# Fourteen dummy matmuls instead of twelve ahead of the first x tile, in a TensorE-bound state-space and expert kernel

## The chip, the cores and the metric

The kernel runs on one core of one Trainium2 chip. The metric is the device time of one execution in microseconds (us). The kernel before took 247.78 us (median of three runs, 247.73 to 248.76).

## The reference, cut to what matters

```python
x = A_x                                              # 1 x 2048 x 1024
g = sigmoid((x * gate_w).sum(-1))
a = ssm(x)        # diagonal complex recurrence over 2048 steps:
                  #   Bu = x @ B_bar^T (real and imaginary plane), h_t = Lam_bar * h_{t-1} + Bu_t
                  #   y  = 2 Re(h @ C^T) + x * Dskip
b = experts(x)    # the 8 tokens with the largest x @ w_r go through a gated MLP; added back to x
return g * a + (1 - g) * b
```

The bulk of the work is two large matrix products: x with the two planes of B (tile `vps`, line 269), and the states with the two planes of C (tile `zps`, line 765). The inputs are bf16. x and B have to be transposed on the way in.

## The kernel before

The large loads of the start are issued from one queue, SyncE's, in this order; only the second plain x tile and the small vectors go through other queues. x is worked on in blocks of 512 rows. The first half of block 0 (two tiles of 128 rows) comes in plain and is transposed on TensorE; the rest of x, B and C are transposed by the DMA.

```python
for tl in range(BPC):                                   # L77: x tiles 0 and 1, plain
    (nc.scalar if tl else nc.sync).dma_start(x0r[:, tl, :], x2d[tl * P:(tl + 1) * P, :])
load_B(0, 0, 1)                                         # L80: real plane of B, row block 0
...
new_X(0)
load_xT(1)                                              # L92: second half of x block 0
load_B(1, 0, 1)                                         # L80: imaginary plane, row block 0
for c0, c1 in ((1, 2), (2, 3), (3, 4), (4, 6), (6, 8)): # the other row blocks, both planes
    for pl in range(2):
        load_B(pl, c0, c1)
```

While the x tiles are on their way, TensorE has nothing to do and multiplies zeros into a PSUM tile that nothing reads. That is the warm-up. It is meant to have TensorE's clock open early. I read the clock from the distance between the starts of two neighbouring 128x256 matmuls: 0.21 us for the dummies in the profile before (the clock is slow, or "cold") and 0.11 us from the first real matmuls on (it is "open").

```python
def warm(n):
    for _ in range(n):
        nc.tensor.matmul(wps[:], lhsT=wt0[:, 0:P], rhs=wt0[:], start=True, stop=True)   # L152, 128x256

warm(12)
for tl in range(BPC):
    ...
    for dc in range(KD):                                # L159: 16 transposes
        nc.tensor.transpose(xq[:, dc, :], x0r[:, tl, dc * P:(dc + 1) * P], ident[:])
    (nc.scalar.copy if tl == 0 else nc.vector.tensor_copy)(out=X[0][...], in_=xq[:])    # L160
warm(2)
... # the three small vectors, L164
warm(1)
s1u(0, 0, 0, 0, 1)    # 8 matmuls: real plane, first half of x
warm(2)
s1u(0, 0, 0, 1, 2)    # 8: real plane, second half of x
s1u(0, 0, 1, 0, 2)    # 8: imaginary plane, both halves
...                   # then two small transposes (vb_ps, L434), then row blocks 1 to 7
```

## Time and profile before

| | before |
|---|---|
| span of the profiled execution | 245.8 us |
| TensorE busy | 239.3 us (97%) |
| VectorE busy | 225.8 us (92%) |
| TensorE waits of more than 0.1 us, all | 1.1 (start), 0.3 (x tile), 0.2 (issue), 0.5 us (B's imaginary plane) |

The span is the time from the first to the last instruction; the device time is some 2 us longer. TensorE is the bound from about 11 us on, so what a change of the start is worth is read from the moment at which TensorE gets into its continuous stream. I use one marker for it: the start of the two small `vb_ps` transposes (L434). They stand in the program right after the first 24 real matmuls (16 of half width and 8 of full width). In the profile before they start at 11.06 us, which leaves 245.8 - 11.06 = 234.7 us for the rest.

### The profile page before, as it was taken

How to read it: one execution, taken by the hardware profiler on the slowest of the kernel's cores; microseconds unless marked ns; L12 is line 12 of the kernel's file. 1: busy time of each engine (PE TensorE's matmuls, PEld its weight loads, DVE VectorE, ACT ScalarE, POOL GpSimd, SP SyncE). 2: the span in 40 equal slices, each digit the busy share in tenths (PEclk: the TensorE clock that was granted, in tenths of full speed). 3: DMA queues.
4: the chain of work that ended last, by engine and by line, in shares of the span. 5: the costliest groups of instructions: out<-in, count | busy, mean ns of one | idle time of the engine just before them, and what ended most of it. 6: DMA issues, size and time to landing. Idle time of an engine off the chain costs nothing.

```text
span 245.8 us, 3504 instructions
## 1 busy us (share of the span) xinstructions
PE 239.3 (97%) x1355; PEld 112.8 (46%) x1379; DVE 225.8 (92%) x229; ACT 119.3 (49%) x205; POOL 26.9 (11%) x47
## 2 busy tenths in 40 slices
PE   7999999999999999999999999999999999999994
PEld 5544444444444444444444444444444444447453
DVE  0889999999999999999999999999999999999952
ACT  3599993233463472323355462235266445456421
POOL 4000000000000300720002030100100211110210
PEclk9999999999999999999999999999999999999999
DMA  8999999999750260577156999778699999942052
GB/s 192 204 156 226 238 237 255 202 241 296 241 169 0 105 153 0 97 160 225 77 192 219 343 264 325 217 239 299 191 347 327 389 293 300 147 65 37 2 132 85
DMA packets 65313, 48.48 MB, mean 197 GB/s; under 512 B 50560, under 2 KB 52224, under 8 KB 65296
## 3 DMA queue, kind: packets, MB, share of 16 engines
q1 hardware_dynamic: 59968, 37.20, 57.8%
q0 software_dynamic: 3264, 7.38, 13.8%
q10 hardware_dynamic: 2064, 3.68, 4.3%
q8 instruction: 11, 0.18, 0.3%
q14 instruction: 6, 0.05, 0.1%
HBM read 27.55 MB, written 8.40 MB: 146 GB/s over the span
## 4 chain that ended last, share of the span: by engine, by line
PE 94%; DMA 2%; SPq 2%; issue 1%; DVE 0%
PE vps L269 44%; PE zps L765 42%; PE zps L781 3%; PE pgu L657 3%; DMA BT<-in_A_B_im_dram 2%; PE y L669 1%; SPq L92 1%; PE zr L483 1%; SPq L80 1%; DVE ot L786 0%; SPq L77 0%; PE xselT_ps L570 0%; PE zs_ps L586 0%; PE zt L490 0%; PE vb_ps L434 0%
## 5 line engine op out<-in xcount | busy, mean ns | idle before, releaser
L269 PE MATMUL vps<-X,BT 128*128 128x512 bf16 (+1 forms) x508 | 111.2, 376 | 1.2 <-DMA BT<-in_A_B_im_dram 0.5
L765 PE MATMUL zps<-CT,H 128*128 128x512 bf16 x469 | 104.4, 379 | 0.6
L269 PEld LDWEIGHTS <-BT 128*128 128x128 bf16 x520 | 50.2, 98 | 60.3 <-issue 1.0
L765 PEld LDWEIGHTS <-H 128*128 128x128 bf16 x480 | 46.5, 98 | 56.6 <-issue 1.3
L306 DVE TENSOR_TENSOR_SCAN U<-d,U 128x2048 bf16<-128x2048 f32 (+2 forms) x22 | 62.0, 2860 | 1.0 <-DVE U L297 0.5
L276 ACT CAST V<-vps 128x512 bf16<-128x512 f32 x64 | 34.3, 588 | 57.7 <-PE vps L269 55.3
L770 ACT ACTIVATE ot<-zps,gcol 128x512 bf16<-128x512 f32 x30 | 20.6, 687 | 46.0 <-PE zps L765 44.8
L739 ACT CAST zps<-xd 128x512 f32<-128x512 bf16 (+1 forms) x29 | 16.6, 576 | 3.9 <-ACT xt L726 2.9
L296 DVE TENSOR_TENSOR V<-V,nTi 128x4096 bf16<-128x4096 bf16 (+2 forms) x11 | 16.7, 1516 | 0.5
L295 DVE TENSOR_TENSOR U<-V,T2tab 128x4096 bf16<-128x4096 bf16 (+2 forms) x11 | 16.6, 1509 | 0.5
L297 DVE TENSOR_TENSOR U<-U,V 128x4096 bf16<-128x4096 bf16 (+2 forms) x11 | 16.7, 1516 | 0.4
L791 POOL DMA_DIRECT2D out_dram<-ot x14 | 13.0, 928 | 30.6 <-ACT ot L770 28.6
L331 DVE TENSOR_TENSOR U<-U,S2tab 128x4096 bf16<-128x4096 bf16 x7 | 16.0, 2292 | 0.2
L333 DVE TENSOR_TENSOR H<-H,U 128x4096 bf16<-128x4096 bf16 x7 | 16.0, 2291 | 0.2
L726 ACT ACTIVATE xt<-xt,omgcol 128x1024 bf16<-128x1024 bf16 x14 | 16.0, 1144 | 0.0
L329 DVE TENSOR_TENSOR H<-U,Ctab 128x4096 bf16<-128x4096 bf16 x7 | 16.0, 2284 | 0.0
L703 POOL DMA_DIRECT2D xt<-in_A_x_dram x12 | 7.2, 596 | 80.6 <-ACT ot L770 22.2
L364 DVE TENSOR_TENSOR_SCAN U<-D,U 128x1024 bf16<-128x1024 f32 x4 | 8.9, 2279 | 0.1
L721 DVE TENSOR_TENSOR xd<-xt,Dbc 128x1024 bf16<-128x1024 bf16 x14 | 9.0, 684 | 0.0
L657 PE MATMUL pgu<-wgu,xsel 128*32 128x448 bf16 x128 | 7.2, 354 | 0.1
L781 PE MATMUL zps<-CT,H 128*128 128x256 bf16 (+1 forms) x47 | 7.1, 307 | 0.1
L716 POOL DMA_DIRECT2D out_dram<-xt x2 | 1.5, 755 | 49.6 <-ACT zps L739 49.6
(152 smaller groups left out, 128.6 us busy)
## 6 DMA issues: line engine op xcount, KB each, us to landing
wgu<-in_B_w_gate_dram SPq DMA_DIRECT2D x16, 448.0 KB, 3.7
wgu<-in_B_w_up_dram SPq DMA_DIRECT2D x16, 448.0 KB, 5.8
out_dram<-ot POOLq DMA_DIRECT2D x14, 256.0 KB, 5.6
wdb<-in_B_w_down_dram SPq DMA_DIRECT2D x7, 512.0 KB, 10.4
xt<-in_A_x_dram POOLq DMA_DIRECT2D x12, 256.0 KB, 4.4
out_dram<-xt ACTq DMA_DIRECT2D x12, 256.0 KB, 5.7
wd<-in_B_w_down_dram SPq DMA_DIRECT2D x5, 512.0 KB, 8.0
xt<-in_A_x_dram SPq DMA_DIRECT2D x4, 256.0 KB, 4.0
```

The costliest lines, as they stand in the source:

```text
L269: nc.tensor.matmul(o, lhsT=BT[pl][:, dc, ct * P:(ct + 1) * P], rhs=X[m][:, dc, k0 * LC:k1 * LC], start=(dc == 0), stop=(dc == KD - 1))
L276: nc.scalar.copy(out=V[k][:, :, ct, :], in_=vp[m, ct][:, :, kk, :])
L295: nc.vector.tensor_tensor(out=u, in0=v, in1=T2tab[:, :, c0:c1, :], op=ALU.mult)
L296: nc.vector.tensor_tensor(out=v, in0=v, in1=bc(nTi, c0, c1), op=ALU.mult)
L297: nc.vector.tensor_tensor(out=u, in0=u, in1=V[k][:, ::-1, c0:c1, :], op=ALU.add)
L306: nc.vector.tensor_tensor_scan(out=fl, data0=d0[:, c0:c1, :].rearrange("p c t -> p (c t)"), data1=fl, initial=0.0, op0=ALU.mult, op1=ALU.add)
L329: nc.vector.tensor_tensor(out=h, in0=g, in1=bc(Ctab, c0, c1), op=ALU.mult)
L331: nc.vector.tensor_tensor(out=g, in0=g, in1=S2tab[:, :, c0:c1, :], op=ALU.mult)
L333: nc.vector.tensor_tensor(out=h, in0=h, in1=G[k][:, ::-1, c0:c1, :], op=ALU.add)
L739: nc.scalar.copy(out=z[:], in_=xd[b][:, d_:d_ + w])
L765: nc.tensor.matmul(zps[:], lhsT=H[k][:, pl, ct, tl * P:(tl + 1) * P], rhs=CT[pl][:, ct, dsl], start=(fresh and ct == 0 and pl == 0), stop= ...
L770: nc.scalar.activation(out=ots[b][:, dsl], in_=zps[:], func=ACT.Copy, scale=gcol[:, b:b + 1])
```

## The change

The intent is to keep TensorE busy until the first x tile has landed, so that no hole is left between warm-up and transposes.

```diff
-    warm(12)
+    warm(14)
```

## The prediction

> **What bounds the kernel now.** I read the chain that ended last first, because it says which engine sets the end and when that engine last waited for something else. Its columns are start (us), length (us), and what.
>
> ```profile
> 0.74 0.40 SPq L77
> ...
> 1.21 1.31 SPq L80
> 2.52 0.05 issue
> 2.57 2.41 SPq L92
> 4.98 0.04 issue
> 5.02 4.16 DMA BT<-in_A_B_im_dram
> 9.18 0.27 issue
> 9.45 1.67 PE vps L269 x7
> ...
> 20.05 10.74 PE vps L269 x49
> ...
> 242.63 0.48 DVE ot L786
> ```
>
> From 9.45 us to about 242.6 us the chain is matmuls on TensorE and short instruction-issue gaps; nothing else stands in it until the last VectorE instruction. Ahead of 9.45 us there is no TensorE work in it at all: there the chain is the SyncE queue issuing loads one after another (x tile, first B transpose, x transpose) and then the landing of the imaginary plane of B, issued at 5.02 us and landed 4.16 us later, at 9.18 us. So the kernel is two pieces: a front of 9.45 us set by loads, and a TensorE-bound rest. Then the waits of TensorE over the whole span (line, what it waited for, us in total, times, longest):
>
> ```profile
> PE wps L152 <- DVE halfpi L132: 1.1, 1, 1.1
> PE vps L269 <- DMA BT<-in_A_B_im_dram: 0.5, 1, 0.5
> PE xq L159 <- DMA x0r<-in_A_x_dram: 0.3, 1, 0.3
> PE vps L269 <- issue: 0.2, 1, 0.2
> ```
>
> These four are all of them. The third is the hole that the change fills, 0.3 us until the x tile has landed. The second comes after it, in front of the real matmuls: TensorE stands still for 0.5 us until B's imaginary plane lands. [...] Last, the timeline of TensorE in the first 9.5 us (start, length, engine, line, operation, tiles, shape, count, idle before):
>
> ```profile
> 1.06 2.74 PE L152 MATMUL wps<-wt 128*128 128x256 bf16 x12 [1.06 <-DVE halfpi L132]
> 4.10 1.89 PE L159 MATMUL xq<-ident,x0r 128*128 128x128 bf16 x16 [0.30 <-DMA x0r<-in_A_x_dram]
> 6.52 0.29 PE L152 MATMUL wps<-wt 128*128 128x256 bf16 x1
> 6.87 1.03 PE L269 MATMUL vps<-X,BT 128*128 128x256 bf16 x8
> ...
> 9.45 0.38 PE L269 MATMUL vps<-X,BT 128*128 128x512 bf16 x1 [0.46 <-DMA BT<-in_A_B_im_dram]
> ```
>
> The first row is the warm-up, the second the 16 transposes of the x tile. They start when the tile lands, not when the warm-up ends. The last row shows the 0.46 us before the first matmul that needs B's imaginary plane.
>
> **What the Trainium skill says.** (1) "Perfetto Trace Analysis", section "Per-instruction lifecycle", for TensorE: the profiled end of a matmul is an estimate that includes the write to PSUM. So a dummy costs the distance to the next start, not its printed duration. The trace agrees: a dummy lasts 418 ns by its row (median of 17), but the first of the twelve starts at 1.06 us and the twelfth at 3.38 us, which is 2.32 / 11 = 0.211 us apart. (2) "TensorE: Matmul & The Clock Gate", Part 1: start-to-start is N / 1.2 GHz while the array is cold and N / 2.4 GHz + 2.5 ns once warm, so for N = 256 an estimate of 213 and 109 ns. The trace agrees on both: 211 ns in the warm-up, and (7.63 - 6.87) / 7 = 109 ns between the first and the eighth start of the first real group. The clock row of the page reads full speed in all forty slices; here I believe the start-to-start distances. (3) The same Part 1: the clock opens after a busy window of about 3.4 us, and the window runs free of the kernel's start. In this trace the dummy at 6.00 us still lasts 0.42 us and the one at 6.52 us lasts 0.29 us, the warm form, so the clock opened between them. (4) The same page, Part 4, says that transposes do not engage the fast clock in the way matmuls do. The transposes here run at (5.7 - 4.1) / 15 = 0.107 us, the cold rate, but the clock opened shortly after, so the trace does not decide it.
>
> **The change part by part.** It removes nothing. It adds two weight loads and two 128x256 matmuls on TensorE, right after the twelve. The comparison of the instruction orders of the two kernels shows no other change on any engine but renumbered tiles: same loads, same queue order, same positions of everything after. The dummies write a PSUM tile that nothing reads; the one instruction that waits for the last dummy of the kernel is a GpSimd memset at 8.18 us, which waits for a later dummy (7.74 us).
> Cost: two matmuls at the cold distance, 2 x 0.211 = 0.42 us of TensorE. Where they lie: the twelfth starts at 3.38 us, so the thirteenth starts at 3.59, the fourteenth at 3.80, and the array takes the next instruction at 4.01 us. The transposes start at 4.10 us because of the load. So 0.42 us of work goes into a hole that by starts is 4.10 - 3.59 = 0.51 us wide (the 0.30 us of the row is counted from the estimated end of the twelfth). About 0.09 us is left: the delay of the transposes is 0, or at most some 0.1 us if the x tile lands earlier than in this execution.
> Sum to the end of the span: 0 from the transposes, and if there is a delay of 0.1 us, it has to pass the wait of 0.46 us at 9.45 us, which nothing on TensorE sets. That leaves 0 for the matmul part of the path. The other way to the end is through the copies of the x tile and the small vectors to VectorE, which is busy 92% of the span. A shift of 0.1 us there would be felt only if TensorE waited for VectorE later, and it does not once in 233 us. So the expected change is 0.0 us.
>
> **The rivals.** (a) The warm-up outlasts the tile. If the load lands 0.2 us earlier in some executions, or if the loads of weights make each dummy dearer, the transposes start 0.1 to 0.3 us late. Against it: the 0.211 us is steady over twelve. Even then the 0.46 us covers it: change 0, at worst +0.1 us. (b) The clock opens earlier. With the hole filled, the 3.4 us window before the transposes holds more work, and in some phases of the window the clock would open at about 4.3 us instead of 7.7. Then 16 transposes take 16 x 0.056 = 0.9 us (the warm figure for N = 128 of Part 1) in place of 1.7, and X is there up to 0.8 us earlier. This is surely what the change is for. For it speaks that the clock is still slow until past 6 us here. Against it: the real matmuls that follow still meet the load that lands at 9.18 us, so TensorE just waits longer, 1.3 us in place of 0.5. Change 0. (c) The clock opens late, in the worst phase at about 1.06 + 2 x 3.4 = 7.9 us. From the timeline, the 16 real half-width matmuls before the wait need 16 x 0.109 = 1.7 us warm and 16 x 0.211 = 3.4 us cold. With the clock opening at 7.9 only the first group of 8, which starts at 6.87 us, would be partly cold: about 5 at 0.211, so some 0.5 us more, just what the wait of 0.46 us covers. If the clock stayed shut through 9.4 us, the front would be about 1.7 - 0.5 = 1.2 us longer, 249.0 us. That is a tail which both kernels have and which the change makes slightly rarer. One of the three runs of before, 248.76, is 1.0 us above the median; I can't tell from one trace if this is it. (d) The two added instructions move the places where TensorE stops for instruction issue, the 0.05 us pieces after every 49 matmuls. Their number does not change: within 0.05 us.
>
> **Range and chances.** All of (a), (b) and (d) end at 0 to 0.1 us; (c) is spread that before has as well. So the predicted time is that of before, 247.8 us. The range is the spread between runs and not the change: three runs of before lie from 247.73 to 248.76, and a median of a few runs in another session may move by some 0.2%. I take 247.3 to 248.5. Two per cent is 5 us, half of the whole front, and the change touches 0.4 us: faster 0.005, same 0.99, slower 0.005.
>
> **What would show it right or wrong.** Right: fourteen dummies from about 1.06 us to about 4.2 us by the rows, transposes starting within 0.1 us of 4.10, no wait for the x tile or one under 0.1 us, the first full-width matmul still at about 9.4 us right after B's imaginary plane lands, and the same 233 us from there to the end. Step (a) is wrong if the transposes start after 4.2 us with the tile long landed. Step (b) shows if the transposes are 0.056 us apart and the wait before 9.4 us has grown by as much. The prediction is wrong if the first full-width matmul moves with the transposes, or if TensorE has a wait for VectorE or ScalarE after 10 us that before had not, or if the load of B's imaginary plane lands at another time than 9.18 us by more than 0.3 us because of the change and not by chance.

## The result, and the profile after

| | before | after |
|---|---|---|
| median, six runs each in the same rounds | 247.55 us | 247.47 us |
| lowest to highest | 246.91 to 248.76 | 247.17 to 247.55 |
| span of the profiled execution | 245.8 us | 245.6 us |
| start of the vb transposes | 11.06 us | 10.76 us |
| rest of the span | 234.7 us | 234.8 us |

The ratio is 0.999 with a 95% interval of 0.9966 to 1.0014. A ratio is the mean time of one kernel's runs over that of the other's of the same rounds, so it is not quite the ratio of the medians in the table.

First TensorE's timeline of the changed kernel for the first 11 us (start, length, engine, line, operation, tiles, shape, count, idle before).

```profile
1.06 3.17 PE L152 MATMUL wps<-wt 128*128 128x256 bf16 x14 [1.06 <-DVE halfpi L132]
4.21 1.89 PE L159 MATMUL xq<-ident,x0r 128*128 128x128 bf16 x16
5.89 0.59 PE L152 MATMUL wps<-wt 128*128 128x256 bf16 x2
...
6.98 1.03 PE L269 MATMUL vps<-X,BT 128*128 128x256 bf16 x8
...
8.06 2.76 PE L269 MATMUL vps<-X,BT 128*128 128x256 bf16 x16
10.76 0.20 PE L434 MATMUL vb_ps<-ident,vrow 8*128 8x8 bf16 x2
```

The fourteen dummies are there and the hole is gone from the matmul rows. The transposes start 0.11 us later than before (4.21 against 4.10 us), and the first row of real matmuls too. But the last group before the vb transposes now runs through: the wait of 0.46 us for B's imaginary plane is gone.

Did the dummies push the transposes? The matmul row cannot tell, because it shows no idle time once the modelled ends overlap. The weight loads can. Here is their timeline in the same window, the kernel before first, then the changed one:

```profile
1.06 2.26 PEld L152 LDWEIGHTS <-wt 128*128 128x128 bf16 x12 [1.06 <-DVE halfpi L132]
4.10 0.98 PEld L159 LDWEIGHTS <-x0r 128*128 128x128 bf16 x10 [0.78 <-DMA x0r<-in_A_x_dram]
```

```profile
1.06 2.69 PEld L152 LDWEIGHTS <-wt 128*128 128x128 bf16 x14 [1.06 <-DVE halfpi L132]
4.21 0.88 PEld L159 LDWEIGHTS <-x0r 128*128 128x128 bf16 x9 [0.45 <-DMA x0r<-in_A_x_dram]
```

In both, the weight load of the first transpose waited for the x tile. The wait shrank from 0.78 to 0.45 us. In this execution the tile simply landed later, 3.4 us after its issue instead of 3.3. So the two dummies lay in the hole and pushed nothing. Nor is this one lucky execution: the fourteenth dummy leaves the array free at 3.81 + 0.21 = 4.02 us, and in all fourteen profiles the first x tile landed at 4.02 to 4.27 us.

Next the chain that ended last in the changed kernel (start, length, what):

```profile
1.06 3.17 PE wps L152 x14
4.23 1.88 PE xq L159 x16
...
6.14 0.69 DVE X L160
...
6.98 1.03 PE vps L269 x8
8.01 0.22 PE wps L152 x2
8.23 2.60 PE vps L269 x16
10.83 0.13 PE vb_ps L434 x2
10.96 48.53 PE vps L269 x224
```

The chain no longer leads through the queue of loads and B's imaginary plane. It leads through the x tile, the transposes, VectorE's copy of the tile and then matmuls. (That it begins with the dummies is an effect of the modelled ends; the weight loads above show the wait for the tile.) The plane of B was issued at 5.14 us and landed 3.4 us later, at about 8.6 us, which is before TensorE wanted it (its first matmul starts at 8.94 us). In the profile before it was 5.02 + 4.16 = 9.18 us. Is that the change, or chance? Nothing in the change touches this load, but that is an argument and not a measurement, so it was the first question for the experiments.

The last row also corrects a reading. There are 224 matmuls in 48.53 us, 0.2167 us each, and no "issue" pieces between them. The pieces of 0.05 us after every 49 matmuls in the profile before were records missing from that trace: (10.74 + 0.05) / 0.2167 = 49.8, so fifty matmuls were there. The header counts say the same: 1355 TensorE instructions before, 1381 after, for a change that adds two. A later look at the unchanged kernel has 1379, and none of these pieces.

### The profile page after: what moved, and what is told of

Same layout as the page of the kernel before. It is cut to its first block, busy times and chain, and to the rows that moved or that the text cites. A ratio compares the mean times of both kernels' runs of the same rounds, so it can differ in the third digit from the quotient of the medians.

```text
span 245.6 us, 3532 instructions
## 1 busy us (share of the span) xinstructions
PE 241.2 (98%) x1381; PEld 113.1 (46%) x1381; DVE 225.8 (92%) x229; ACT 119.1 (48%) x205; POOL 26.8 (11%) x47
## 4 chain that ended last, share of the span: by engine, by line
PE 98%; DVE 1%; issue 0%
PE vps L269 45%; PE zps L765 42%; PE zps L781 3%; PE pgu L657 3%; PE wps L152 1%; PE y L669 1%; PE xq L159 1%; PE zr L483 1%; DVE X L160 0%; DVE ot L786 0%; PE xselT_ps L570 0%; PE zs_ps L586 0%; PE zt L490 0%; DVE wt L129 0%; PE vb_ps L434 0%
```

## The experiments

Twelve kernels were run, timed in up to five rounds beside the kernel before on the same chip. Two theories stood at the start. Mine: the dummies lie in a hole, and what moves the front from execution to execution is the landing of loads and the moment at which the clock opens. The rival: the change itself moved something (the landing of B, or the clock) and is worth 0.1 to 0.3 us.

### 1. The kernel before against itself, and the changed kernel again

No edit in either.

> The kernel before, unchanged, timed against itself: the noise floor. Theory (the dummies fill a hole and the front is set by loads whose landing varies): ratio 1.000 within 0.002, and the profile lands B's imaginary plane somewhere between 8.4 and 9.3 us, with the start of the first full-width matmul either at about 8.9 us (landing before it is needed) or 0.27 us after the landing. Rival (the change itself moved that landing from 9.18 to 8.5 us): the landing is again at 9.1 to 9.2 us here.

> The changed kernel again. Theory: ratio 0.998 to 1.001; the transposes start with the landing of the x tile (4.1 to 4.2 us), the clock opens at about 6.3 us, the landing of B's imaginary plane anywhere from 8.4 to 9.3 us. Rival (the change is a real gain of 0.1 to 0.3 us by an earlier landing): ratio 0.9990 or less with the landing at 8.5 us again.

> One more look at the kernel before for where the clock opens and where the loads land. Theory (the time of opening is a matter of chance between 4.2 and 7 us): the transposes are either 0.107 or 0.056 us apart, and the span less the start of the vb transposes is 234.8 us within 0.1. Rival (twelve dummies always open it at the same time): as in the first look, 6.3 us.

Measured: the kernel before against itself gave 247.35 against 247.52 us, ratio 1.0003 (0.9965 to 1.0041). The changed kernel gave 247.58 us in the same rounds, ratio 0.9997 (0.9967 to 1.0027). So an interval of five rounds is about 0.7% wide here, and an effect of 0.1 us (0.04%) cannot be seen in times. It can be bounded in traces. TensorE's timeline of the first look at the unchanged kernel:

```profile
4.24 1.07 PE L159 MATMUL xq<-ident,x0r 128*128 128x128 bf16 x16 [0.44 <-DMA x0r<-in_A_x_dram]
...
6.18 1.03 PE L269 MATMUL vps<-X,BT 128*128 128x256 bf16 x8 [0.25 <-DVE vec L165]
7.05 0.38 PE L152 MATMUL wps<-wt 128*128 128x256 bf16 x2
7.38 1.03 PE L269 MATMUL vps<-X,BT 128*128 128x256 bf16 x8
8.94 1.67 PE L269 MATMUL vps<-X,BT 128*128 128x512 bf16 x7 [0.52 <-DMA BT<-in_A_B_im_dram]
10.54 0.20 PE L434 MATMUL vb_ps<-ident,vrow 8*128 8x8 bf16 x2
```

Here the sixteen transposes take 1.07 us instead of 1.89, so the clock was open at 4.24 us, with twelve dummies. B's imaginary plane landed at 8.67 us (issued at 5.22, 3.44 us to land). In the second look (state unknown, being a single run) the plane landed in time, at 8.65 us, and the transposes were slow again:

```profile
4.22 1.89 PE L159 MATMUL xq<-ident,x0r 128*128 128x128 bf16 x16 [0.42 <-DMA x0r<-in_A_x_dram]
...
8.08 2.76 PE L269 MATMUL vps<-X,BT 128*128 128x256 bf16 x16
10.77 0.20 PE L434 MATMUL vb_ps<-ident,vrow 8*128 8x8 bf16 x2
```

What follows: the early landing of B comes without the change, so the rival is refuted on that point. Of the thirteen profiles that load B's first row block in this order, with whatever number of dummies, eleven have the plane landed at 8.39 to 8.84 us. The late ones are the profile before (9.18) and that of joinB below (9.51), two of the seven with twelve dummies, too few to tie a late landing to the number of dummies. The moment at which the clock opens varies by some 2 us between executions of one and the same kernel (before 4.24 us in the first look; in the second, dummies at 5.90 and 6.12 us are still 0.21 us apart). And in the first look it is seen what an early clock is worth: the real matmuls start at 6.18 instead of 6.87 us, then TensorE waits for B all the same, 0.52 us. The gain at the vb transposes is 11.06 - 10.54 = 0.5 us, which is the difference of the two landings (9.18 against 8.67), not of the clock.

### 2. No dummies, eighteen, thirty-two

```diff
-    warm(12)
+    warm(0)      # warm0;   warm(18): warm18;   warm(32): warm32
```

> No dummies ahead of the x tile (12 removed, the five later ones stay). Theory (the warm-up opens the clock in time and the last two dummies don't matter for that): the transposes start at 4.1 us as before, the clock opens 1 to 3.5 us later than 6.3 us, so some of the 16 half-width matmuls run 0.211 us apart, and the time rises by 0.5 to 1.5 us (ratio 1.002 to 1.006). Rival (the whole warm-up is hidden behind the loads, so its length never matters): ratio 1.000.

> Eighteen dummies in the warm-up, six more than before, past the landing of the x tile. Theory: the warm-up ends by starts at 4.6 to 4.9 us, the x transposes are 0.4 to 0.7 us later than the landing, and the two vb transposes start at 10.6 to 11.3 us (the later where the clock opens only at 6.4 us); the rest of the span from there is 234.8 us as in the traces so far, so the span is 245.4 to 246.1 and the ratio 0.999 to 1.002. Rival (each dummy past the landing costs 0.211 us): 0.8 us more than before, ratio 1.003 or more.

> Thirty-two dummies in the warm-up, 20 more than before. Theory (dummies cost nothing until they outlast the landing and then the 0.46 us wait): the warm-up ends near 7.2 us (25 dummies 0.211 us apart until the clock opens at about 6.4 us, 7 at 0.109), the transposes are 3 us late but 0.056 us apart, first real matmul at about 9.1 us instead of 6.9, the time rises by 1.3 to 2.0 us (ratio 1.005 to 1.008). Rival (each dummy costs its distance of 0.211 us from the first on): 4.2 us more. Rival (the start-up is hidden altogether): 0.

| kernel | median (before, same rounds) | ratio, 95% interval | transposes start | vb transposes | rest of span |
|---|---|---|---|---|---|
| 0 dummies | 248.65 (247.52) | 1.0028 (0.9999 to 1.0058) | 4.11 | 10.96 | 235.0 |
| 18 dummies | 247.44 (247.37) | 1.0002 (0.9968 to 1.0036) | 4.88 | 10.68 | 234.8 |
| 32 dummies | 248.80 (247.52) | 1.0048 (1.0018 to 1.0077) | 6.46 | 12.18 | 234.8 |

With none, the clock opened at about 7.5 us. TensorE's timeline has the first eight real matmuls in 1.34 us instead of 1.03:

```profile
6.87 1.34 PE L269 MATMUL vps<-X,BT 128*128 128x256 bf16 x8
```

The first and the last of them start at 6.87 and 7.94 us, which is what three cold distances among seven would make (3 x 0.211 + 4 x 0.109 = 1.07 us). The median rose by 1.1 us as expected, but the interval just touches 1, and the profiled execution is one of the two quick ones (247.77 us; the other four timed at 248.63 to 248.88). So this one trace shows a clock that opens later than in any look with dummies (at most about 6.7 us), and not the source of all of the 1.1 us. The rest of the span in this look is 0.2 us longer, part of it a wait of 0.16 us behind the vb transposes.

With eighteen, the transposes start 0.7 us later than the tile, and it costs nothing that can be seen. In this execution the clock opened at about 5.0 us, so the transposes took 1.14 us, and that won back what the six dummies had taken.

With thirty-two the front is longer and the time rises by 1.3 us, where twenty more dummies at the cold distance would have been 4.2 us. Dummies that outlast the tile are paid for, but only partly: the later thirteen of them ran with the open clock, and the transposes behind them too. The expected range of 1.3 to 2.0 us was just met, but not as expected: the clock opened at about 5.0 us instead of 6.4, so the transposes started at 6.46 us and the real matmuls at 8.39, where 7.2 and 9.1 us had been put down.

```profile
1.06 5.56 PE L152 MATMUL wps<-wt 128*128 128x256 bf16 x32 [1.06 <-DVE halfpi L132]
6.46 1.06 PE L159 MATMUL xq<-ident,x0r 128*128 128x128 bf16 x16
```

### 3. Twenty dummies where TensorE is the bound

```diff
     s1(0, 2)
+    wmid = ps_m.tile([P, LC], F32, name="wmid", tag="m")
+    for _ in range(20):
+        nc.tensor.matmul(wmid[:], lhsT=ident[:], rhs=X[0][:, 0, 0:LC], start=True, stop=True)
```

> Twenty extra matmuls of the dummies' shape (128x256) not in the warm-up but after the third pair of real groups, in the TensorE-bound part at about 18 us, where the clock is open. Theory (a dummy costs its distance to the next start wherever TensorE sets the end, and nothing ahead of a load): 20 x 0.109 = 2.2 us more, ratio 1.009, with no change of the front (the two vb transposes start at 10.5 to 11.1 us as in the traces so far). Rival (dummies are cheap anywhere, filled in between weight loads): under 1 us. For comparison, 20 extra at the start cost 1.3 us.

Measured: 249.35 against 247.37 us, ratio 1.0068 (1.0038 to 1.0098), 2.0 us more by the medians and 1.7 us (0.9 to 2.4) by the ratio, where 2.2 us was expected. The timeline:

```profile
14.79 3.19 PE L269 MATMUL vps<-X,BT 128*128 128x512 bf16 x14
17.81 2.35 PE L446 MATMUL wmid<-X,ident 128*128 128x256 bf16 x20
20.00 4.26 PE L269 MATMUL vps<-X,BT 128*128 128x512 bf16 x19
```

From the first added matmul to the next real one are 20.00 - 17.81 = 2.19 us, 0.109 us each, and the rest of the span behind the vb transposes (10.76 us) is 247.7 - 10.76 = 236.9 instead of 234.8 us. So by the trace a dummy costs its distance where TensorE sets the end, and the times agree within their interval. The same instruction is free ahead of a load. That is the contrast on which the prediction rested.

### 4. Loads in another order

```diff
-    load_xT(1)
     load_B(1, 0, 1)
+    load_xT(1)
...
     s1u(0, 0, 0, 0, 1)
-    warm(2)
+    s1u(0, 0, 1, 0, 1)
     s1u(0, 0, 0, 1, 2)
-    s1u(0, 0, 1, 0, 2)
+    s1u(0, 0, 1, 1, 2)
```

> Twelve dummies as before; the transpose of B's imaginary plane is issued ahead of that of x's second half, and the four half-width groups go real, imaginary, real, imaginary, without the two dummies between. Theory (the front is set by the loads of the SyncE queue, and the order of two of them matters more than the dummies): no wait for B's imaginary plane, at most a wait for x's second half until 8.5 to 8.7 us, the two vb transposes at 10.3 to 10.6 us, span 245.0 to 245.4, ratio 0.998 to 1.000. Rival (the front is set by the copies of the x tile and the matmuls, the loads are incidental): vb transposes at 10.6 us or later.

The edit also removes the two dummies between the half-width groups. Measured: 247.77 against 247.37 us, ratio 0.9998 (0.9967 to 1.0028). The expectation was a shorter front; it was not. TensorE's timeline:

```profile
6.57 2.00 PE L269 MATMUL vps<-X,BT 128*128 128x256 bf16 x16 [0.29 <-DVE vec L165]
9.21 1.91 PE L269 MATMUL vps<-X,BT 128*128 128x256 bf16 x16 [0.64 <-DMA X<-in_A_x_dram]
11.05 0.20 PE L434 MATMUL vb_ps<-ident,vrow 8*128 8x8 bf16 x2
```

The second half of x, now issued at 4.08 us, took 5.1 us to land. TensorE waits for it instead of for B. Swapping two loads on one queue swapped one wait for another. There was a second finding, in the chain that ended last of this look (the slowest of the six runs, 248.25 us): the start is followed not by matmuls but by load after load, up to the imaginary plane of B's row blocks 4 and 5, which landed at 23.9 us and held TensorE up once more (the rest of the span is 235.4 us).

```profile
14.83 4.43 SPq L80
19.26 0.04 issue
19.30 4.60 DMA BT<-in_A_B_im_dram
23.90 0.05 issue
23.95 36.43 PE vps L269 x168
```

The second look at the kernel before has the same load just in time, as TensorE's weight loads show. The wait of 0.37 us in the last field was still covered by the matmuls in flight.

```profile
23.11 1.84 PEld L269 LDWEIGHTS <-BT 128*128 128x128 bf16 x10 [0.37 <-DMA BT<-in_A_B_im_dram]
```

### 5. The supply of B, and the slow tail

Some runs of the kernel before lie 1 to 2 us above its median: over all rounds 10 of 46 runs were above 248.5 us. A new theory: they are executions in which the load just named lands late. If so, smaller loads should remove them and a larger one should cost on every run.

```diff
-    for c0, c1 in ((1, 2), (2, 3), (3, 4), (4, 6), (6, 8)):
+    for c0, c1 in ((1, 2), (2, 3), (3, 4), (4, 5), (5, 6), (6, 8)):   # splitB, splitB_b; splitB14 has warm(14) as well
+    for c0, c1 in ((1, 2), (2, 3), (3, 4), (4, 8)):                    # joinB
```

> Twelve dummies as before; the B transposes of row blocks 4 and 5, which before loads as one pair (4 to 6), go as two pairs. Theory (the runs of before above 248.5 us, some 6 of 34, and no dummies, come from the imaginary plane of blocks 4 to 6 landing after the 23.1 us at which TensorE wants it; in the looks so far it lands at 22.4 to 23.1 us): block 4's imaginary plane lands 1 us or more earlier, no weight load waits for B at 23 us, no run is above 248.3 us, median 247.2 to 247.4. Rival (slow runs come from elsewhere): one or two of the six runs above 248.5 us, as in before.

> splitB once more, for its spread. Theory: again no run above 248.3 us, so none of twelve, where before has some one in six. Rival: one to three of the twelve above 248.5 us.

> The same with fourteen dummies. Theory (dummies thirteen and fourteen lie in the hole, and the load of B was the one other wait near the front): median within 0.2 us of splitB, no run above 248.3 us. Rival (the dummies gain where the second wait is away): 0.2 us or more under splitB.

> Twelve dummies; row blocks 4 to 8 of B in one pair of transposes. Theory (the supply of B is the limit of the first 25 us with no slack): the imaginary plane lands 2 to 4 us later than 23.1 us, TensorE waits for it, the median rises by 1.5 to 4 us (ratio 1.006 to 1.016). Rival (there is slack in the supply): within 0.3 us of before.

| kernel | median (before: 247.64) | lowest to highest | ratio, 95% interval |
|---|---|---|---|
| splitB | 247.22 | 247.14 to 248.89 | 0.9979 (0.9946 to 1.0013) |
| splitB again | 247.31 | 247.14 to 247.91 | 0.9972 (0.9944 to 1.0000) |
| splitB, 14 dummies | 247.57 | 247.16 to 248.01 | 0.9976 (0.9948 to 1.0005) |
| joinB | 252.92 | 250.97 to 253.78 | 1.0189 (1.0149 to 1.0230) |

The larger load costs 5.3 us by the medians (4.7 by the ratio), more than the 1.5 to 4 expected; it is slower beyond doubt, though the interval leaves open whether by 2%. I had reckoned with the imaginary plane only, but the real one came late as well. The weight loads of joinB show both, and the two waits make 5.15 us:

```profile
23.62 1.41 PEld L269 LDWEIGHTS <-BT 128*128 128x128 bf16 x8 [2.06 <-DMA BT<-in_A_B_re_dram]
28.11 3.78 PEld L269 LDWEIGHTS <-BT 128*128 128x128 bf16 x19 [3.09 <-DMA BT<-in_A_B_im_dram]
```

So the supply of B has next to no slack around 23 us. With the smaller loads no weight load waits for B there in any of the three looks. But the theory of the slow runs is not upheld as the only cause: one run of splitB took 248.89 us. Over the three kernels that is 1 run of 18 above 248.5 us, against 10 of 46 of the kernel before, too few to say that the slow runs have become rarer. And the look at splitB with fourteen dummies happened to be one of its slower executions (247.99 us). Its vb transposes start at 10.67 us, as early as any, but the rest of the span is 235.5 us. TensorE's timeline, and then that of the load queue, say why:

```profile
60.18 1.69 PE L483 MATMUL zr<-X,rg 128*32 128x512 bf16 x28 [0.54 <-DMA X<-in_A_x_dram]
```

```profile
36.61 6.96 SPq L108 DMA_TRANSPOSE CT<-in_A_C_im_dram  x1
43.69 4.90 SPq L92 DMA_TRANSPOSE X<-in_A_x_dram  x2
48.63 4.46 SPq L108 DMA_TRANSPOSE CT<-in_A_C_re_dram  x1
53.18 4.35 SPq L92 DMA_TRANSPOSE X<-in_A_x_dram  x2
```

The same entries of the load queue in the profile before:

```profile
33.95 4.14 SPq L108 DMA_TRANSPOSE CT<-in_A_C_im_dram  x1
38.20 6.17 SPq L92 DMA_TRANSPOSE X<-in_A_x_dram  x2
44.41 4.44 SPq L108 DMA_TRANSPOSE CT<-in_A_C_re_dram  x1
48.95 4.17 SPq L92 DMA_TRANSPOSE X<-in_A_x_dram  x2
```

The last two transposes of x were issued from 53.18 us on, before from 48.95. The last of them landed at about 60 us, and TensorE's gate product waited for it, 0.54 us by the matmul row and 0.8 us by the weight loads. Of the 4.2 us by which the queue was late, 2.7 were there when the chunk of C began (36.61 against 33.95 us), and that chunk added 2.8 by taking 6.96 us to issue instead of 4.14; the next pair won 1.3 back.

The chain that ended last in this look names something else, VectorE:

```profile
52.32 2.30 DVE U L295
54.62 0.49 SPq L92
55.16 4.98 DMA X<-in_A_x_dram
```

The queue's own rows speak against it. The first load of the pair starts right behind the chunk of C before it (48.63 + 4.46 = 53.09 us), so nothing was waited for ahead of it, and the VectorE instruction named ends during its issue. That issue took 1.93 us; in the profile before it took 1.94 us although another VectorE instruction is named there, and in the second look at splitB 1.85 us with a third one. The releaser is inferred from an update that fell into the issue, not from a pause.

So a late queue can reach TensorE as far on as 60 us, which is one slow execution explained. But the smaller loads have a part in it: in the three looks with them this pair went out at 50.57, 52.43 and 53.18 us, at 48.22 to 48.95 us in the five looks at the two kernels of the change, and at 51.14 at the latest in looks at other kernels with the loads of B as before. In the second look at splitB it landed at 59.5 us, just as TensorE came to it. So splitting B won slack at 23 us and seems to have lost some at 60 us, and this execution does not tell what makes runs of the kernel before slow. The slowest of them (up to 249.57 us) remain open, as none fell on a profile.

Is splitB better than both kernels? Its two medians are 0.3 to 0.4 us under the kernel before of the same rounds. The intervals reach 1.0013 and 1.0000. I would keep it only with an eye on the loads at 60 us; it is not shown to be faster. Fourteen dummies on top of it changed nothing that can be told (0.9976 beside 0.9979 and 0.9972; the median is 0.35 us above splitB's where 0.2 was expected, within the spread of the runs).

## Why the prediction was right

- **The time.** 247.47 us lies in the range of 247.3 to 248.5, 0.3 us under the point. The kernel before was itself lower in the same rounds (247.55 instead of 247.78), so most of the 0.3 us is the session and not the change.
- **The cost of the two dummies and where they lie** was right. The fourteenth starts at 3.81 us (predicted 3.80), and the weight load of the first transpose still waited 0.45 us for the tile in one look at the changed kernel and 0.40 us in the other. Both dummies are in the hole. The transposes started 0.11 us after the 4.10 us of the prediction because the tile landed that much later.
- **Rival (a), the warm-up outlasting the tile**, did not happen. The cover that I gave against it was weaker than I wrote. I said that the 0.46 us before the first full-width matmul would take up a delay. In both looks at the changed kernel, and in the second look at the kernel before, that wait does not exist: B's imaginary plane landed before it was needed, and the path led from the x tile through transposes and copies. A delay of the transposes would have gone straight into the front there. That the first full-width matmul would start at about 9.4 us, right after that landing, was wrong for the profile after: it started at about 8.9 us without a wait. The step that failed is the sentence that the front is "a front of 9.45 us set by loads". Two of three looks at the unchanged kernel had TensorE wait for B's plane, until 9.45 and 8.94 us; the third had no such wait. The start of the vb transposes in them is 11.06, 10.54 and 10.77 us, and two different paths set it.
- **Rival (b), an early clock hidden behind B**, was right in mechanism: it was seen in an unchanged kernel, with the transposes 0.056 us apart and the wait for B still there. That the two dummies would make it likelier is not shown. Over the looks with twelve dummies the clock opened from before 4.24 to about 6.6 us, over the three with fourteen from about 4.9 us (splitB14, whose transposes turn from 0.107 to 0.056 us apart there) to 6.7 us (the second look at the changed kernel, in which the dummy at 6.56 us lasts 0.36 us, between the 0.42 of a cold and the 0.28 of an open clock).
- **Rival (c), the late clock as the cause of 249 us**, was not seen. With twelve dummies or more no look had the clock open later than about 6.7 us. Among the kernels that time like the kernel before, two profiles fell on slower executions, 248.25 us (bim_first) and 247.99 us (splitB14). They had it open at about 5.3 and 4.9 us and lost time at 24 and 60 us. A slow run of the kernel before was never profiled.
- **Rival (d)** was a misreading without consequence: the 0.05 us pieces are missing records and not stops for instruction issue.
- **VectorE.** I argued that a shift of VectorE is felt only where TensorE waits for it. A wait could also go from VectorE through a buffer to the load queue and from there to TensorE, which I passed over. No run here shows such a wait. The view of the queue's waits in the kernel before lists 1.5 us for VectorE ahead of the load of x for the gate, but, as in experiment 5, the load starts without a pause and its issue is no longer for it. With the change the rest of the span is 234.8 us in both looks.

In short, the 0.0 us was right because of the hole. The second cover that I counted on is there only in some executions.

## What to carry to other kernels

An instruction that fills a hole in front of a load costs nothing: the traces show it for 0.42 us of dummies, while the ratio of 0.999, with an interval of half a per cent, could not have told 0.42 us (0.17%) from nothing. And the same kind of instruction costs its full distance where its engine sets the end (20 x 0.109 us, 2.0 us measured). Before trusting a second wait as cover, look at several executions: a wait of half a microsecond for a load may be gone in the next one. And cut the span at one fixed instruction; "start of the vb transposes" plus a rest that was 234.7 to 234.9 us in nine of the fourteen profiles told more here than any timing, whose interval was about 0.7% wide.

## What the Trainium skill lacked or had wrong

- "TensorE: Matmul & The Clock Gate", Part 4, says that the fast clock does not engage for transposes. Here sixteen transposes ran 0.056 us apart in the first look at the unchanged kernel (1.07 us in all) and 0.107 us apart in others (1.89 us): the open clock holds for them as for matmuls. (The kernel calls the transpose with an identity, as the page describes it; the trace lists it as MATMUL and does not show the mode.) They may also count as activity, which one look suggests and none tests: with no dummies ahead the clock opened at about 7.5 us, 3.4 us after the first transpose, though half of that time was transposes.
- The same page, Part 1, gives the transition as varying by about half a microsecond between runs, and elsewhere in the part as run-variable without a figure in time. Here it came from under 3.2 to about 5.6 us after the first dummy. The page speaks of unbroken activity: the two looks without a hole (18 and 32 dummies) have about 3.9 us, as it says; the spread comes from looks in which TensorE waited for the tile.
- "DMA: Bandwidth & Descriptors" does not tell how much the landing of one DMA transpose varies. The same 256 KB of B's imaginary plane landed 3.2 to 4.4 us after issue over the looks that issue it third of the transposes, and the issue of the same chunk of C took 4.14 us in one look and 6.96 us in one at another kernel. These variations are larger than the change studied.
- No page says that missing matmul records show up in a chain of waits as short "issue" pieces: 1355 records and 1379 in two looks at the same kernel.
